# Exponentials, norm sums, weight sums and loads in other slots at the start of the second batch of a fused attention and GEGLU kernel

## The chip, the cores and the metric

The kernel runs on one core of one Trainium2 chip. The metric is the device time of one execution in microseconds, the median of several runs. The core has five engines that each work through an instruction list of their own in order: PE (TensorE, matrix products), DVE (VectorE), ACT (ScalarE), POOL (GpSimd) and SP (SyncE, here the issuer of most DMA transfers). They wait for each other on semaphores.

## The reference

An efficient attention (softmax over the features for q, over the sequence for k) feeds a GEGLU feed-forward block. Cut to what is computed:

```python
# q, k, v: (8, 8, 576, 64); w_gate, w_val: (512, 1536); w_out: (1536, 512)
q_s = exp(q - max(q, -1)) / (sum over the last axis + 1e-9)
k_s = exp(k - max(k, 2))  / (sum over the sequence + 1e-9)
kv  = einsum('bhsd,bhse->bhde', k_s, v)
x   = einsum('bhsd,bhde->bhse', q_s, kv)     # then (8 * 576, 512)
g   = x @ w_gate
out = (0.5 * g * (1 + erf(g / sqrt(2))) * (x @ w_val)) @ w_out
```

## The kernel before

Eight batches are worked one after the other. In each, 512 of the 576 rows form a main block; the 64 rows that are left of every batch are collected in `xtr` and form one more block of 512 rows. The order of blocks is 0 to 6, then the collected block, then 7. What this document calls block b is the feed-forward work on batch b.

**Attention of one batch.** q, k and v are loaded into fp32 tiles (`ld_b`: two buffers for q, two for k, one for v). ACT takes `exp` of q into `eq` and of k into `ek` (L178; two buffers each, by the parity of the batch). Each of four head pairs of `eq` is then normalised by `norm`: DVE sums and takes a reciprocal (`norm_sum`, L196 and L198), and POOL or DVE multiplies (`norm_mul`, L215). `cast_v` turns v into fp16 (L154 on POOL). `unit_kv` or `unit_kv4` forms k times v on PE. The normalised q has to be transposed: in batches 0 and 1 by PE (`unit_t`), with the left rows by a DMA (`unit_trem`, L337, tile `eqtr`), and from batch 2 by one DMA transpose of all of `eq` (`unit_td`, L344, tile `eqt`). `unit_x` or `unit_x4` multiplies with kv into PSUM tiles `psx` and `psxr`, and ACT and DVE copy these to `xt` and `xtr` (L156, L158).

**Feed-forward of one block.** Twelve tiles (`fi` 0 to 11) of 128 hidden features each: four matmuls into `psg` and four into `psv` (L425), then `gate`: Gelu on ACT (L430, into one of three buffers `gl`) and a product on DVE (L431, into `ht`). Six PSUM banks go round in a ring for `psg` and `psv`. In blocks 0 and 1 the first two or three tiles are interleaved with the last work on `xt` (`ffn_first0`, `ffn_first`): their first two matmuls of each product need only head pairs 0 and 1.

The product with w_out in blocks from 1 on is a Strassen form (`out_strassen`, L546): seven half-size products, which need sums of blocks of w_out (`tw[1]` to `tw[4]`, made once by `sum_w`, L515, on DVE) and of `ht` (`sum_h`, L532, for each block, on DVE, made between the tiles from 7 on). Product 1 uses `ht` tiles 0 to 5, product 2 uses 6 to 11, products 5 and 6 use sums, product 4 is the last before the next block's tiles.

**What sets the order.** `plan` is a table written out by hand: `at(b, FI, i, ...)` hangs work behind tile i of block b, `at(b, NS, i, ...)` at places in the product with w_out, and `ride` runs it there. What hangs there is put into the lists of the engines at that place, and so a plan entry sets the order on each engine, but not across them. SP's list holds loads, transposes and stores in order too, so that a transfer which has to wait (for a buffer to come free, or for its source) keeps the later ones waiting.

**Tables of ACT.** Gelu and Exp do not share a table. Wherever ACT changes from one to the other an ACT_TABLE_LOAD appears in the trace. `preload` (L420) runs the function on one element, to bring its table in early.

**Around the change.** In the kernel before, ACT changes to Gelu at the end of block 0's product with w_out (`at(0, NS, 7, preload)`). In block 1, tile 3 is followed by w_out sums 3 and 4, Exp of q2 (q of batch 2) and norm 0 of batch 2; tiles 4 to 6 by norms 1 to 3; tile 7 by the first half of Exp of k2 and the casts of v2; tile 9 by the DMA transpose of batch 2; tile 11 by the loads of q, k and v of batch 3, the second half of Exp of k2, Exp of q3 and k3, `exp_rem0` (Exp of batch 0's left rows) and the casts of v3. w_out sums 1 and 2 stand inside `ffn_first`.

Of the kernel before, what the change touches and what calls it, by code (L numbers as in the profile page):

```python
# [11 lines left out]
ACTF = mybir.ActivationFunctionType  # L12
ALU = mybir.AluOpType
# [5 lines left out]
def kernel(  # L19
# [10 lines left out]
    nc = tc.nc  # L30

    B, H, S, D = q.shape
# [4 lines left out]
    NFI = F // P  # L37
# [469 lines left out]

    tw = {}

    def sum_w(i):  # L510
        t = wstp.tile([P, NO, 256], f16, name=f"tw{i}", tag="wst")
        b11, b12 = wo_sb[:, 0:NO, 0:256], wo_sb[:, 0:NO, 256:512]
        b21, b22 = wo_sb[:, NO:NFI, 0:256], wo_sb[:, NO:NFI, 256:512]
        a, b = {1: (b12, b11), 2: (b22, tw.get(1)), 3: (b22, b12), 4: (b21, tw.get(2))}[i]
        nc.vector.tensor_tensor(out=t, in0=a, in1=b, op=ALU.subtract)  # L515
        tw[i] = t

    sh = {}
# [203 lines left out]
    FI, NS = 0, 1  # L722
    plan = {}

    def at(b, kind, i, *fns):
        plan.setdefault((b, kind, i), []).extend(fns)

    L = lambda f, *a: (lambda: f(*a))
# [5 lines left out]
    at(0, NS, 5, L(unit_t, 1, 0))  # L734
    at(0, NS, 16, L(unit_kv, 1, 0), L(cast_v, 1, 4, 8), L(load_batch, 2, ((v, "v"),)),
       L(norm, 1, 3))
    at(0, NS, 17, L(unit_x, 1, 0, "act", True), L(unit_x, 1, 1, "act", True))
    at(0, NS, 7, L(preload, ACTF.Gelu))
    first1 = [[L(unit_t, 1, 1), L(unit_kv, 1, 1)], [L(unit_x, 1, 2, "act"), L(sum_w, 1)],
              [L(unit_x, 1, 3, "dve"), L(sum_w, 2)]]  # L740

    def x_upper0():
        unit_x(0, 2, "act")
# [3 lines left out]


    at(1, FI, 2, L(unit_trem, 1))
    at(1, FI, 3, L(sum_w, 3), L(sum_w, 4), L(exp, "q", 2), L(norm, 2, 0, "pool"))  # L750
    at(1, FI, 4, L(norm, 2, 1, "pool"))
    at(1, FI, 5, L(norm, 2, 2, "pool"))
    at(1, FI, 6, L(norm, 2, 3, "pool"))
    at(1, FI, 7, L(exp, "k", 2, 0, 4), L(cast_v, 2, 0, H))
    at(1, FI, 9, L(unit_td, 2))
    at(1, FI, 11, L(load_batch, 3), L(exp, "k", 2, 4, 8), L(exp, "q", 3), L(exp, "k", 3), L(exp_rem0), L(cast_v, 3, 0, H))
    at(1, FI, 4, make_s)
    at(1, NS, 2, L(unit_kv4, 2))
    at(1, NS, 4, L(unit_x4, 2, ("act", "dve"), 1))
    at(2, FI, 7, L(norm_rem0))  # L760
    at(3, FI, 8, L(unit_trem, 0))
    for b in range(2, B):
        if b + 2 < B:
            at(b, FI, 0, L(load_batch, b + 2, ((v, "v"), (q, "q"), (k, "k"))))
            at(b, FI, NFI - 1, L(exp, "q", b + 2), L(exp, "k", b + 2))
            vcast = L(cast_v, b + 2, 0, H)
        if b + 1 < B:
            n = b + 1
            for hp in range(HP):
                at(b, FI, hp, L(norm_sum, n, hp), L(norm_mul, n, hp, "pool"))  # L770
            at(b, FI, 4, L(unit_td, n))
            if n + 1 < B:
                at(b, FI, 4, vcast)
            if n == 3:
                at(b, FI, 5, L(unit_kv4, n))
            at(b, NS, 4, L(unit_x4, n, ("act", "dve"), 0 if n == 4 else None))
            if n + 1 < B:
                at(b, NS, 4, L(unit_kv4, n + 1, n == 4))
# [67 lines left out]
```

## Time and profile before

The median of three runs is 308.58 us (308.30 to 308.87). The profiled execution spans 309.0 us at a mean granted PE clock of 0.994.

| engine | busy us | share of the span | instructions |
|---|---|---|---|
| PE | 295.9 | 96% | 2077 |
| DVE | 204.1 | 66% | 392 |
| ACT | 146.0 | 47% | 195 |
| POOL | 74.3 | 24% | 83 |

The page of a profile gives such totals, a strip of the span in 40 slices, the chain of work that ended last and the costliest groups of instructions. Further views are drawn from the trace: a timeline (start, duration, engine, line, operation, what it writes and reads, count, and in brackets the idle time ahead of it with what ended it), a table by stretches of time (for each stretch its length, the busy time of PE, weight load, DVE, ACT and POOL with the count of instructions, the granted PE clock, the share of the DMA engines and GB/s), and the list of waits. Where PE is busy nearly everywhere, as here, the reader looks for the stretches where it is not, or where its clock is below 1.00, and asks in the timeline what it waited for there. Block 0's product with w_out ends at about 48.6 us, block 1's tiles run from there to about 71.4, its product with w_out to about 83.7, and block 2 follows.

### The profile page before, as it was taken

The numbers are of one execution on the slowest core, as the hardware profiler recorded it, in microseconds if no ns is written. First come the engines' busy times: TensorE is split into PE (matmuls) and PEld (weight loads), VectorE is DVE, ScalarE is ACT, GpSimd is POOL, SyncE is SP. The second block draws the span as 40 slices with busy tenths as digits, with TensorE's granted clock in tenths as the row PEclk, the third lists the DMA queues.
The fourth block names the chain that finished last, engine by engine and source line by source line (L and its number), as shares of the span: only waits on it lengthen the run. The fifth ranks groups of instructions, "written<-read, shape, count | busy, mean of one in ns | idle before, by whom it ended". The sixth has DMA issues, their size and how long they took to land.

```text
span 309.0 us, 5369 instructions
## 1 busy us (share of the span) xinstructions
PE 295.9 (96%) x2077; PEld 167.6 (54%) x2077; DVE 204.1 (66%) x392; ACT 146.0 (47%) x195; POOL 74.3 (24%) x83
## 2 busy tenths in 40 slices
PE   3999999998889999999999999999999999999994
PEld 1444455445634486448644764477447644774473
DVE  2944388789737785868586848685868545834672
ACT  3763465994663385338533844384431333123320
POOL 2667461073058000720063005400510000000000
PEclk9999999999979999999999999999999999999999
DMA  6999999709959303980399029801140110022003
GB/s 224 372 383 392 401 387 387 210 0 227 379 175 377 71 0 138 367 187 0 124 345 215 1 102 341 240 0 77 61 85 3 81 57 0 0 69 69 1 2 136
DMA packets 54762, 51.66 MB, mean 167 GB/s; under 512 B 18513, under 2 KB 50769, under 8 KB 54737
## 3 DMA queue, kind: packets, MB, share of 16 engines
q1 hardware_dynamic: 53152, 49.75, 49.9%
q10 hardware_dynamic: 1584, 1.57, 1.6%
q8 instruction: 16, 0.26, 0.4%
q14 instruction: 10, 0.07, 0.1%
HBM read 37.75 MB, written 9.44 MB: 153 GB/s over the span
## 4 chain that ended last, share of the span: by engine, by line
PE 89%; DMA 5%; POOL 1%; SPq 1%; ACT 1%; DVE 1%; issue 1%; POOLq 0%; ACTq 0%
PE psg L425 30%; PE psv L425 30%; PE psa L546 12%; PE psc L546 6%; PE psy L493 3%; PE psb L546 3%; DMA vt<-in_v_dram 3%; DMA qt<-in_q_dram 2%; PE pskv L301 1%; SPq L134 1%; POOL v L154 1%; PE pst L326 1%; PE psx L388 1%; PE psx L367 1%; POOL eq L215 1%
## 5 line engine op out<-in xcount | busy, mean ns | idle before, releaser
L431 DVE SCALAR_TENSOR_TENSOR ht<-psv,gl 128x512 f16<-128x512 f32 x108 | 73.7, 685 | 67.6 <-PE psv L425 49.1
L430 ACT ACTIVATE gl<-psg 128x512 f32<-128x512 f32 x108 | 63.3, 598 | 98.1 <-PE psg L425 96.5
L425 PE MATMUL psg<-xt,wg_sb 128*128 128x512 f16 x384 | 101.6, 382 | 2.0 <-ACT xt L156 1.9
L425 PE MATMUL psv<-xt,wv_sb 128*128 128x512 f16 x384 | 101.4, 382 | 0.5 <-DVE ht L431 0.5
L425 PEld LDWEIGHTS <-wv_sb 128*128 128x128 f16 x432 | 42.4, 98 | 52.0 <-issue 2.2
L425 PEld LDWEIGHTS <-wg_sb 128*128 128x128 f16 x432 | 42.3, 98 | 51.7 <-issue 3.5
L215 POOL TENSOR_TENSOR eq<-eq,rrq 128x640 f16<-128x640 f16 (+1 forms) x27 | 34.4, 1276 | 125.6 <-issue 92.3
L546 PEld LDWEIGHTS <-ht 128*128 128x128 f16 x384 | 37.1, 98 | 8.6 <-DVE ht L431 1.5
L196 DVE TENSOR_REDUCE rq<-eq 128x10 f32<-128x640 f16 x28 | 22.7, 810 | 2.9 <-ACT eq L178 2.9
L546 PE MATMUL psa<-tw,ht 128*128 128x256 f16 x192 | 23.6, 273 | 0.2 <-DVE yo L578 0.2
L154 POOL CAST v<-vt 128x640 f16<-128x640 f32 x26 | 18.5, 754 | 14.7 <-DMA vt<-in_v_dram 14.7
L178 ACT ACTIVATE eq<-qt 128x2560 f16<-128x2560 f32 (+2 forms) x10 | 18.5, 1864 | 6.5 <-DMA qt<-in_q_dram 6.4
L178 ACT ACTIVATE ek<-kt 128x1280 f16<-128x1280 f32 (+1 forms) x11 | 19.1, 1748 | 5.0 <-DMA kt<-in_k_dram 5.0
L546 PEld LDWEIGHTS <-sh 128*128 128x128 f16 x192 | 18.8, 98 | 2.2
L628 ACT ACTIVATE yo<-psa 128x512 f32<-128x512 f32 (+1 forms) x8 | 4.6, 570 | 19.4 <-PE psa L546 19.4
L546 PE MATMUL psb<-wo_sb,ht 128*128 128x256 f16 x96 | 12.1, 273 | 1.0 <-DVE ht L431 0.9
L572 DVE TENSOR_SCALAR sn<-psa 128x512 f32<-128x512 f32 (+1 forms) x16 | 10.5, 654 | 3.9 <-PE psa L546 3.9
L425 PE MATMUL psg<-xtr,wg_sb 128*128 128x512 f16 x48 | 12.3, 379 | 0.0
L425 PE MATMUL psv<-xtr,wv_sb 128*128 128x512 f16 x48 | 12.3, 379 | 0.0
L546 PE MATMUL psc<-wo_sb,s 128*128 128x256 f16 x96 | 11.8, 273 | 0.0
L546 PE MATMUL psa<-tw,sh 128*128 128x256 f16 x96 | 11.8, 273 | 0.0
L546 PE MATMUL psa<-wo_sb,ht 128*128 128x256 f16 x96 | 11.8, 273 | 0.0
(86 smaller groups left out, 251.4 us busy)
## 6 DMA issues: line engine op xcount, KB each, us to landing
out_dram<-yo SPq DMA_DIRECT2D x15, 512.0 KB, 3.5
kt<-in_k_dram SPq DMA_DIRECT2D x7, 640.0 KB, 8.3
vt<-in_v_dram SPq DMA_DIRECT2D x7, 640.0 KB, 5.3
qt<-in_q_dram SPq DMA_DIRECT2D x7, 640.0 KB, 6.8
qt<-in_q_dram SPq DMA_DIRECT2D x8, 512.0 KB, 7.3
wost<-in_moe_w_out_dram SPq DMA_DIRECT2D x6, 512.0 KB, 7.9
kt<-in_k_dram SPq DMA_DIRECT2D x6, 512.0 KB, 9.2
vt<-in_v_dram SPq DMA_DIRECT2D x6, 512.0 KB, 5.9
```

The source lines that it names most:

```text
L134: (nc.scalar if b == 0 and t == 1 else nc.sync).dma_start(out=tiles[(nm, b)][t:P:2, h0:h1, c0 * D:NC * D], in_=src[b, h0:h1].rearrange("h ...
L154: nc.gpsimd.tensor_copy(out=dst, in_=src)
L178: nc.scalar.activation(out=dst[:, n0:NC, h0 * D:h1 * D].rearrange(o, d=D, **({"t": 2} if b >= QUAD else {})), in_=heads(tiles[(nm, b)], b, ...
L196: nc.vector.reduce_sum(rq, e, axis=mybir.AxisListType.X)
L215: (nc.gpsimd if eng == "pool" else nc.vector).tensor_tensor(out=e, in0=e, in1=rrq.unsqueeze(-1).to_broadcast((P, n, 2, D)), op=ALU.mult)
L425: nc.tensor.matmul(ps, w[:, ci, fi * P:(fi + 1) * P], xt[:, ci, :], start=(ci == 0), stop=(ci == HP - 1))
L430: nc.scalar.activation(out=gl, in_=psg, func=ACTF.Gelu)
L431: nc.vector.scalar_tensor_tensor(out=ht[:, fi, :], in0=psv, scalar=_H_SCALE, in1=gl, op0=ALU.mult, op1=ALU.mult)
L493: nc.tensor.matmul(psy, ht[:, fi, ns * P:(ns + 1) * P], wo_sb[:, fi, :], start=(fi == 0), stop=(fi == NFI - 1))
L546: nc.tensor.matmul(ps[t], a, w, start=(first and j == 0 and (t == ts[0] or ps[t].tensor is not ps[ts[0]].tensor)), stop=(j == NO - 1), ski ...
L572: nc.vector.tensor_scalar(out=sn[:, t], in0=src, scalar1=1.0 / _H_SCALE, scalar2=None, op0=ALU.mult)
L628: nc.scalar.activation(out=yo[1][:, t, c[0]], in_=src, func=ACTF.Copy, scale=1.0 / _H_SCALE)
```

## The change

Work on batches 2 and 3 that rides in block 1 is put into other slots:

- Exp of q2 takes the place of the Gelu preload at the end of block 0, while the Exp table is still in; the preload goes behind the copy of head pair 2 in `ffn_first`.
- Norms 0 and 1 of batch 2 go into `ffn_first`, norms 2 and 3 behind tiles 3 and 4.
- Sums 1 and 3 of w_out go to POOL, at the end of block 0; sums 2 and 4 stay on DVE, behind tiles 5 and 6.
- q and k of batch 3 are loaded from tile 3 of block 1 instead of tile 11; v of batch 3 stays at tile 11.
- The two halves of Exp of k2 go behind tiles 4 and 8 (before: 7 and 11), the casts of v2 behind 5, the transpose of batch 2 behind 8.
- Exp of batch 0's left rows goes from the end of block 1's tiles to the end of block 2's, and its norm from tile 7 of block 2 to tile 5 of block 3.

It is meant to have batch 3's q and k in place before ACT wants them, and to take work out of block 1's tiles.

```diff
-    def sum_w(i):
+    def sum_w(i, eng="dve"):
...
-        nc.vector.tensor_tensor(out=t, in0=a, in1=b, op=ALU.subtract)
+        (nc.gpsimd if eng == "pool" else nc.vector).tensor_tensor(out=t, in0=a, in1=b, op=ALU.subtract)
...
-    at(0, NS, 17, L(unit_x, 1, 0, "act", True), L(unit_x, 1, 1, "act", True))
-    at(0, NS, 7, L(preload, ACTF.Gelu))
-    first1 = [[L(unit_t, 1, 1), L(unit_kv, 1, 1)], [L(unit_x, 1, 2, "act"), L(sum_w, 1)],
-              [L(unit_x, 1, 3, "dve"), L(sum_w, 2)]]
+    at(0, NS, 17, L(unit_x, 1, 0, "act", True), L(unit_x, 1, 1, "act", True), L(sum_w, 1, "pool"),
+       L(sum_w, 3, "pool"))
+    at(0, NS, 7, L(exp, "q", 2))
+    first1 = [[L(unit_t, 1, 1), L(unit_kv, 1, 1)],
+              [L(unit_x, 1, 2, "act"), L(preload, ACTF.Gelu), L(norm, 2, 0, "pool")],
+              [L(unit_x, 1, 3, "dve"), L(norm, 2, 1, "pool")]]
...
     at(1, FI, 2, L(unit_trem, 1))
-    at(1, FI, 3, L(sum_w, 3), L(sum_w, 4), L(exp, "q", 2), L(norm, 2, 0, "pool"))
-    at(1, FI, 4, L(norm, 2, 1, "pool"))
-    at(1, FI, 5, L(norm, 2, 2, "pool"))
-    at(1, FI, 6, L(norm, 2, 3, "pool"))
-    at(1, FI, 7, L(exp, "k", 2, 0, 4), L(cast_v, 2, 0, H))
-    at(1, FI, 9, L(unit_td, 2))
-    at(1, FI, 11, L(load_batch, 3), L(exp, "k", 2, 4, 8), L(exp, "q", 3), L(exp, "k", 3), L(exp_rem0), L(cast_v, 3, 0, H))
-    at(1, FI, 4, make_s)
+    at(1, FI, 3, L(norm, 2, 2, "pool"), L(load_batch, 3, ((q, "q"), (k, "k"))))
+    at(1, FI, 4, L(exp, "k", 2, 0, 4), L(norm, 2, 3, "pool"), make_s)
+    at(1, FI, 5, L(sum_w, 2), L(cast_v, 2, 0, H))
+    at(1, FI, 6, L(sum_w, 4))
+    at(1, FI, 8, L(exp, "k", 2, 4, 8), L(unit_td, 2))
+    at(1, FI, 11, L(load_batch, 3, ((v, "v"),)), L(exp, "q", 3), L(exp, "k", 3), L(cast_v, 3, 0, H))
     at(1, NS, 2, L(unit_kv4, 2))
     at(1, NS, 4, L(unit_x4, 2, ("act", "dve"), 1))
-    at(2, FI, 7, L(norm_rem0))
+    at(3, FI, 5, L(norm_rem0))
...
-            at(b, FI, NFI - 1, L(exp, "q", b + 2), L(exp, "k", b + 2))
+            at(b, FI, NFI - 1, L(exp, "q", b + 2), L(exp, "k", b + 2), *([exp_rem0] if b == 2 else []))
```

## The prediction, made before the change was run

> **What bounds the kernel now.** I read the page first: PE is busy 296 of 309 us, so only idle PE, or PE at a lower clock, can give time back. Its row of slices and the clock row beneath show where (a slice is 309.0/40 = 7.72 us):
>
> ```profile
> PE   3999999998889999999999999999999999999994
> PEclk9999999999979999999999999999999999999999
> ```
>
> Slices 9 to 11 (70 to 93 us) hold the only 8s after the start, and slice 11 the only low clock. The table by stretches, with PE busy as its second number and the clock as the third from the end, resolves them:
>
> ```profile
> 68.00:72.00 4.00, 3.55 (x20) 1.78 (x19) 3.97 (x6) 2.80 (x5) 4.00 (x5) 1.00 0.57 106
> 72.00:76.00 4.00, 3.01 (x27) 2.23 (x25) 3.86 (x10) 1.78 (x2) 0.29 (x1) 1.00 0.93 221
> ...
> 84.00:85.70 1.70, 0.00 (x0) 0.00 (x0) 0.33 (x1) 1.70 (x6) 0.22 (x1) 1.00 0.50 202
> 85.70:87.00 1.30, 1.14 (x5) 0.48 (x5) 0.00 (x0) 0.97 (x2) 1.30 (x3) 1.00 0.02 9
> 87.00:89.00 2.00, 2.00 (x7) 0.69 (x5) 0.00 (x0) 1.87 (x2) 1.21 (x2) 0.54 0.55 223
> 89.00:91.00 2.00, 2.00 (x7) 0.75 (x6) 1.63 (x3) 0.61 (x2) 0.00 (x0) 0.60 0.57 115
> ```
>
> Two losses. The first is the end of block 1's tiles: the PE timeline has psv of tile 11 waiting for DVE ht near 70.1 and psb waiting for the last ht near 74.3. Tile 11 began at 69.08; with 1.73 us for a tile, 1.31 for product 1 and 10 x 0.109 ahead of psb's last pair, that pair was due at 73.21 and began at 75.15: **1.94 us**. The second is the passage to block 2. There product 4 ends near 83.73 (82.42 + 12 x 0.109), but four groups of block 2, at 0.864 each, end only at 91.15 instead of 83.73 + 3.46 = 87.19: **3.96 us**, of which about 2.0 idle, 0.15 a second short wait, 1.8 half clock.
>
> Who causes the passage? The ACT timeline:
>
> ```profile
> 78.39 2.34 ACT L178 ACTIVATE eq<-qt 128x2560 f16<-128x2560 f32 x1 [4.60 <-DMA qt<-in_q_dram]
> 81.95 2.34 ACT L178 ACTIVATE ek<-kt 128x2560 f16<-128x2560 f32 x1 [1.22 <-DMA kt<-in_k_dram]
> 84.19 0.61 ACT L223 ACTIVATE eq0r<-q0r 64x512 f16<-64x512 f32 x1
> 84.71 0.51 ACT L156 CAST xtr<-psxr 128x128 f16<-128x128 f32 x2
> 85.12 1.06 ACT L156 CAST xt<-psx 128x512 f16<-128x512 f32 x2
> ```
>
> The xt copies that start block 2 stand behind Exp of q3 and k3, which wait for their loads. Those loads are late because the DMA queue stands behind a transposing DMA, and that behind batch 2's norms:
>
> ```profile
> 68.80 3.08 SPq L344 DMA_TRANSPOSE eqt<-eq  x1
> 71.93 1.29 SPq L134 DMA_DIRECT2D qt<-in_q_dram  x2
> 73.27 1.66 SPq L134 DMA_DIRECT2D kt<-in_k_dram  x2
> 75.03 1.94 SPq L134 DMA_DIRECT2D vt<-in_v_dram  x2
> ```
>
> The chain of waits names vt in this stretch; the timeline decides, since the Exps wait for qt and kt.
>
> **What the Trainium skill says.** "TensorE: Matmul & The Clock Gate", What's actually happening: half rate after an idle window of about 3.4 us, full rate after as much busy time. The trace agrees on half (0.50 between 88 and 90 us) and on the recovery (about 3.6 us); here about 2 us of idleness was enough. "ScalarE: Activation LUTs", What ACT_TABLE_LOAD costs: 1283 ns plus a drain of about 1380. The trace shows 1.28 us and the next ACTIVATE at once, so I count 1.28. "GPSIMD Engine Reference", 4.1 Engine selection: two-input elementwise work is about 2x slower than on DVE. The rows show 1.26 against 0.82 us for norm's product. The same page, 1 Specifications: the SBUF interface is shared with DVE instructions that have two SBUF inputs. The trace agrees: the sums of ht (L532) take 0.42 us from 100 to 240, but 1.12, 0.82 and 0.94 beside POOL work at 67.9 to 71.7.
>
> **The change part by part.**
>
> *q and k of batch 3 queued at tile 3.* Their buffers were last read by Exp of q1 and k1, done at 47.1, so SP issues them right after the eqtr transpose (52.8 to 54.2). The DMA engines are full until 58.3 and idle until 68.8, so 2.36 MB at the 386 GB/s seen there take 6.1 us: landed near 64.5. The Exps then follow tile 11's Gelu: 71.7 + 1.28 + 2 x 2.34 = 77.7, well before the first psxr (81.6). exp_rem0 (0.61) leaves this point; at block 2's end ACT waited 2.44 for psxr, which hides it. ACT is ready for xt, and DVE's two xt copies end at 84.33 against a need at 83.73 + 3 x 0.215 = 84.38: nothing left, or 0.1. With the idle gone I expect the clock to stay up, as between blocks 2 and 3. **Gain 3.9.**
>
> *Exp of q2 in the place of the Gelu preload.* ACT is free at 49.45, but q2's second half was issued at about 42.7 and took
>
> ```profile
> qt<-in_q_dram SPq DMA_DIRECT2D x1, 512.0 KB, 7.4
> ```
>
> so it lands at 50.1, and Exp runs 50.3 to 52.6. Behind it on ACT stands the copy of psx for head pair 2 (51.80 before): it ends near 53.2, and PE wants it at 52.68. **Loss 0.55.** On DVE norm sum 0 waits for the same Exp (52.6 + 0.81 + 0.22 = 53.7), then the xt copy of pair 3 ends at 54.4; PE, already late, wants it at 54.5. The preload (1.28 + 0.20) ends at 54.7, before gate 0 needs it (54.39 + 0.55). The count of table loads from 49 to 88 us stays seven.
>
> *Sums 1 and 3 on POOL.* 1536 elements at 1.26/640 us each: 3.0 us (estimate; the GPSIMD page's 4497 ns for 2048 fp32 gives 3.4). Two from 48.8 end at 54.8 to 55.6. Beside them DVE mostly reads PSUM or one SBUF input; norm 3 of batch 1 (1.16, already beside POOL) may grow by 0.3, but the wait for q2 absorbs that. Queued behind on POOL: norms 0 and 1 (to 57.3), norm 2, norm 3 (to 62.3: ht4 60.2 on DVE, 1.03 for its sum, 1.26 on POOL), cast of v2 (to 65). No PE work asks for these before 78. DVE loses 2 x 0.95 us of work.
>
> *Sums 2 and 4 after tiles 5 and 6.* DVE idles for Gelu 5 until 63.7 (next part). From there four ht at 0.65, sums 2 and 4 at 0.95, two pairs of ht sums (0.85, 0.75) end at 69.8: before ht9 can start at 70.5. Nothing.
>
> *Exps of k2 after tiles 4 and 8.* Each costs ACT 2 x 1.28 + 1.27 = 3.83 us against 1.73 us of PE per tile, and ACT spends 0.6 a tile, so the first is caught up by tile 8. PSUM holds three tiles, so no psg waits; the first ends at 63.1. The second: Gelu 8 ends at 66.1, Gelu 9 starts at 69.95. DVE then has ht9 (70.5), two sums (0.80), ht10 (0.62), two sums (0.67), ht11: done 70.5 + 3.5 = 74.0. PE wants it at 73.21 + 0.55 = 73.76: a wait of 0.24 if nothing disturbs the sums.
>
> *v of batch 3.* It still stands behind the transpose (62.3 now) and the cast of v2. Before, q3, the first thing after the transpose, landed 9.4 us after the transpose's issue, so v3 lands at about 71.7 and POOL casts it until 75, beside exactly those sums. One sum at 0.94 instead of 0.42 adds 0.5; if v3 lands a microsecond earlier, up to 1.6; later than 73.5, nothing. I take 0.5: ht11 at 74.5 instead of 75.15, **gain 0.65**, with the q2 loss and all else ahead of it inside (1.15 at best with that loss, -0.45 at worst).
>
> *norm_rem0 and the rest.* 1.54 us of DVE move from tile 7 of block 2 to tile 5 of block 3, where norms 0 to 3 have finished; the transpose that needs it is issued after tile 8. Nothing, as DVE ran through the same in block 2 without a PE stall.
>
> **Sum.** 0.65 + 3.96 - 0.1 = 4.5: 308.6 - 4.5 = **304.1**. From block 2 on, the order of work is as before, and nothing in it waited for what moves.
>
> **The rivals.** (a) *Undisturbed*: q2 lands in time and v3 after the tight sums: ht11 at 74.0 - 0.55 = 73.45, gain 1.7 + 3.9 = 5.6, **303.0**. For it: the landing is known to 0.2 us only. (b) *The wait is handed on*: q2 costs 1.0 and v3's cast 1.6, ht11 at 74.0 + 0.45 + 1.6 = 76.05: -0.9 + 3.9 = 3.0, **305.6**; the stretched sums near 68 us speak for it. (c) *The clock falls anyway*, because the waits near 53 and 74 or the thin 64x64 matmuls suffice: 4.5 - 1.8 = 2.7, **305.9**. Against it: the waits near 74 left it at 1.00 before. (d) *Slower*: ACT is in order, and Exp of q2 now stands ahead of block 1's first Gelu. If it started 5 us later than I compute (the queue is full until 58.3), PE would idle some 5.5 us and run cold for another 1.8, and the ht waits would stay: 308.6 - 3.9 + 7.3 = **312**. Against it: the 7.4 us above.
>
> **How the numbers follow.** My forecast 0.55, (a) 0.18, (b) 0.14, (c) 0.09, (d) 0.04. The range of 302.8 to 306.1 takes in (a) to (c), with 0.2 beyond the outer two for the repeat scatter (308.3 to 308.87), and leaves out (d) and halves of the tails. Faster 0.95, within 0.2% 0.01, slower 0.04.
>
> **What would show it.** PE at 1.00 clock and without a gap over 0.2 us where block 2 begins; Exp of q3 and k3 back to back from 72 us with no DMA wait; one PE wait of about 0.5 us for ACT xt near 52.7; sums of w_out on POOL at 3 us; ht11 done near 74.5 us, with L532 rows stretched beside the cast of v3. The forecast is wrong if the passage keeps its low clock, or if PE waits over 1 us in block 1's first three tiles.

## The result, and the profile after

The changed kernel takes **307.15 us** (306.90 to 307.24), against 308.61 us for the kernel before beside it: a ratio of 0.9952, with a 95% interval of 0.9935 to 0.9969. It is faster, by 1.46 us, but that is a third of the 4.5 us that were forecast (304.1), and the time lies outside the range of 302.8 to 306.1.

The strips of the page of after answer to those of before; a slice is now 305.4/40 = 7.64 us:

```profile
PE   3999999999999999999999999999999999999994
PEclk9999999999999999999999999999999999999998
```

The three 8s and the 7 of the clock row are gone. (The new 8 at the end of the clock row costs nothing: it lies behind 302 us, where PE has no work left.) The spans seem to say that 309.0 - 305.4 = 3.6 us were won, but the times say 1.46. Setting each profiled execution's span against its own time explains it: an execution is timed some 1.8 us above its span (307.19 for the 305.4 of after), and the execution of before whose trace the prediction was read from was timed at 310.83 us, 2.2 above the median of its own kernel. This trace cannot be compared with that of after as it stands; experiment e1 has a typical one.

Block 1's end in after, on the PE timeline (start, duration, instruction, count, and in brackets the idle time with what ended it):

```profile
74.20 0.39 PE L546 MATMUL psb<-wo_sb,ht 128*128 128x256 f16 x2 [0.25 <-DVE ht L431]
74.43 1.47 PE L546 MATMUL psc<-tw,sh 128*128 128x256 f16 x12
76.11 1.47 PE L546 MATMUL psa<-tw,sh 128*128 128x256 f16 x12 [0.21 <-DVE sn L572]
...
78.63 1.47 PE L546 MATMUL psc<-wo_sb,s 128*128 128x256 f16 x12 [0.30 <-DVE sn L572]
...
82.19 1.47 PE L546 MATMUL psa<-tw,ht 128*128 128x256 f16 x12
83.50 1.03 PE L425 MATMUL psg<-xt,wg_sb 128*128 128x512 f16 x4
...
114.17 0.82 PE L301 MATMUL pskv<-v,ek 128*64 128x65 f16 x40 [0.45 <-ACT xt L156]
```

The wait for the last ht has shrunk, and block 2 follows product 4 without a gap (82.19 + 1.31 = 83.50). Three waits in these lines are new: two for `sn` (a DVE result from a PSUM tile that PE uses again) in block 1's product with w_out, and one ahead of `pskv`, the k times v product of batch 4, at the end of block 2.

ACT and SP do what they were meant to do. In the ACT timeline Exp of q3 and k3 run back to back with no wait for a load. In the SP timeline their loads stand ahead of the transpose:

```profile
72.92 2.34 ACT L178 ACTIVATE eq<-qt 128x2560 f16<-128x2560 f32 x1
75.16 2.32 ACT L178 ACTIVATE ek<-kt 128x2560 f16<-128x2560 f32 x1
81.75 0.53 ACT L156 CAST xtr<-psxr 128x128 f16<-128x128 f32 x2 [4.26 <-PE psxr L398]
```

```profile
54.35 1.67 SPq L134 DMA_DIRECT2D qt<-in_q_dram  x2
56.06 3.22 SPq L134 DMA_DIRECT2D kt<-in_k_dram  x2
62.66 4.97 SPq L344 DMA_TRANSPOSE eqt<-eq  x1
67.73 1.29 SPq L134 DMA_DIRECT2D vt<-in_v_dram  x2
```

### The profile page after: what moved, and what is told of

Same layout as the page of the kernel before. It is cut to its first block, busy times and chain, and to the rows that moved or that the text cites. A ratio compares the mean times of both kernels' runs of the same rounds, so it can differ in the third digit from the quotient of the medians.

```text
span 305.4 us, 5368 instructions
## 1 busy us (share of the span) xinstructions
PE 294.4 (96%) x2077; PEld 167.7 (55%) x2077; DVE 201.7 (66%) x390; ACT 145.9 (48%) x195; POOL 81.6 (27%) x85
## 4 chain that ended last, share of the span: by engine, by line
PE 72%; DVE 1%; ACT 0%; issue 0%
PE psg L425 24%; PE psv L425 24%; PE psa L546 13%; PE psc L546 6%; PE psb L546 3%; PE pskv L301 1%; PE psx L388 1%; DVE yo L578 0%; PE psxr L388 0%; DVE s L532 0%; DVE sn L572 0%; ACT xt L156 0%; DVE yo L624 0%; DVE ht L532 0%; ACT xtr L156 0%
## 5 line engine op out<-in xcount | busy, mean ns | idle before, releaser
L425 PE MATMUL psg<-xt,wg_sb 128*128 128x512 f16 x384 | 100.5, 379 | 0.3 <-ACT xt L156 0.3
L154 POOL CAST v<-vt 128x640 f16<-128x640 f32 x26 | 19.3, 783 | 9.5 <-DMA vt<-in_v_dram 9.5
L156 ACT CAST xtr<-psxr 128x128 f16<-128x128 f32 (+1 forms) x8 | 2.1, 290 | 21.9 <-PE psxr L388 15.1
L417 PE MATMUL pswarm<-warm,ident 128*128 128x512 f16 x20 | 7.3, 525 | 4.9 <-ACT warm L676 4.9
```

The costliest lines, as they stand in the source:

```text
L154: nc.gpsimd.tensor_copy(out=dst, in_=src)
L417: nc.tensor.matmul(ps, ident, warm, start=True, stop=True)
L425: nc.tensor.matmul(ps, w[:, ci, fi * P:(fi + 1) * P], xt[:, ci, :], start=(ci == 0), stop=(ci == HP - 1))
```

## The experiments

### e1: the kernel before once more

No edit.

> The kernel before, unchanged, for the clock of its executions. Theory A: the half clock of 1.8 us at the passage to block 2 belonged to the one profiled execution of before (309.0 us span, 310.8 us timed, 2.2 above the median). Then most executions span about 306.8 us at a clock above 0.997, and a trace of one shows only some 2.1 us lost at the passage. Rival B: the clock falls there in every execution; then spans stay near 309 with a clock near 0.994, and the change loses its gain elsewhere.

Measured: 308.55 us (308.25 to 308.93), ratio 0.9993 (0.9981 to 1.0004). The trace is of an execution of 308.58 us: span 306.8, clock 1.000. The passage on its PE timeline:

```profile
82.40 1.47 PE L546 MATMUL psa<-tw,ht 128*128 128x256 f16 x12
85.17 1.29 PE L425 MATMUL psg<-xt,wg_sb 128*128 128x512 f16 x4 [1.29 <-ACT xt L156]
86.29 1.03 PE L425 MATMUL psv<-xt,wv_sb 128*128 128x512 f16 x4
...
88.88 1.03 PE L425 MATMUL psg<-xt,wg_sb 128*128 128x512 f16 x4
```

The three groups behind the first take 2.59 us (86.29 to 88.88), 0.86 each, so none runs at half clock, and the table by stretches has the clock at 1.00 from 68 to 96 us. In the first trace the same three groups took 4.27 us (86.88 to 91.15). Product 4 ends at 83.71; four groups should end at 87.17 and end at 88.88: the passage costs **1.71 us, not 3.96**. Theory A holds; the 2.1 us that it set for the passage were 0.4 too many. The first trace shows a kind of execution that comes up now and then: of the 80 executions of before recorded with the experiments, 4 took 310.78 to 310.86 us at a mean clock of 0.994, and none of the others more than 309.35 us.

With this trace the three can be laid side by side (start of an instruction, us):

| PE begins | before, first trace | before, e1 | after | after gained on e1 |
|---|---|---|---|---|
| psb's last pair, block 1 | 75.15 | 75.13 | 74.20 | 0.93 |
| product 3, block 1 | 78.85 | 78.83 | 78.63 | 0.20 |
| product 4, block 1 | 82.42 | 82.40 | 82.19 | 0.21 |
| tile 2 of block 2 | 91.15 | 88.88 | 86.95 | 1.93 |
| tile 0 of block 3 | 119.93 | 117.65 | 116.25 | 1.40 |
| span | 309.0 | 306.8 | 305.4 | 1.4 |

Gained: 0.93 at the last ht, 1.72 at the passage. Given back: 0.73 between psb and product 3, and 0.53 in block 2. The sum, 1.39, comes close to the 1.46 that was timed.

### e2: the loads alone

```diff
-    at(1, FI, 3, L(sum_w, 3), L(sum_w, 4), ...
+    at(1, FI, 3, L(load_batch, 3, ((q, "q"), (k, "k"))), L(sum_w, 3), L(sum_w, 4), ...
-    at(1, FI, 11, L(load_batch, 3), ...
+    at(1, FI, 11, L(load_batch, 3, ((v, "v"),)), ...
```

> Before with one part of the change alone: q and k of batch 3 queued behind tile 3 of block 1. Theory A: the idle time at the passage (2.0 + 0.15 us) goes and nothing else moves: 308.6 - 2.1 = 306.5 us, with no wait of ACT for q3 or k3. Rival B (half clock regularly lost before): 308.6 - 3.9 = 304.7 us. Rival C: the transpose of batch 2, now behind two loads in the queue, comes late and takes part of the gain: 307 to 308 us.

Measured: 306.93 us, ratio 0.9947 (0.9934 to 0.9960), a gain of 1.68, where e1's passage costs 1.71. In the PE timeline psb's last pair begins at 75.10, as in before, and block 2 follows product 4 without a gap:

```profile
82.37 1.47 PE L546 MATMUL psa<-tw,ht 128*128 128x256 f16 x12
83.68 1.03 PE L425 MATMUL psg<-xt,wg_sb 128*128 128x512 f16 x4
```

So this part gains the passage and nothing else, and alone it is no slower than the whole change.

### e3: v of batch 3 later

```diff
-    at(1, FI, 11, L(load_batch, 3, ((v, "v"),)), L(exp, "q", 3), L(exp, "k", 3), L(cast_v, 3, 0, H))
+    at(1, FI, 11, L(exp, "q", 3), L(exp, "k", 3))
-    at(1, NS, 4, L(unit_x4, 2, ("act", "dve"), 1))
+    at(1, NS, 4, L(unit_x4, 2, ("act", "dve"), 1), L(load_batch, 3, ((v, "v"),)), L(cast_v, 3, 0, H))
```

> After, with load and cast of v of batch 3 moved behind product 7 of block 1. Theory: the cast on POOL at 74.2 to 77.4 us stretched two ht sums on DVE (0.82 and 0.89 instead of 0.42 us), which made PE wait twice for sn in block 1's product with w_out. Without it the L532 rows are all at 0.42 to 0.43, both waits go, and the time is 0.5 to 0.7 us below after: about 306.5 us. Rival: the waits come from the order on DVE and stay: 307.15 us. Second rival: v of batch 3 then comes late for block 2: above 307.2 us.

Measured: 306.38 us, ratio 0.9927 (0.9915 to 0.9939), 0.77 below after. First come the POOL and DVE timelines of after in the stretch concerned, then two of the rows of L532, the sums of ht, in e3 (min/median/max in ns):

```profile
74.20 3.16 POOL L154 CAST v<-vt 128x640 f16<-128x640 f32 x4 [8.19 <-DMA vt<-in_v_dram]
```

```profile
74.17 0.42 DVE L532 TENSOR_TENSOR sh<-ht 128x512 f16<-128x512 f16 x1
74.63 0.82 DVE L532 TENSOR_TENSOR sh<-sh,ht 128x512 f16<-128x512 f16 x1
75.38 0.68 DVE L572 TENSOR_SCALAR sn<-psa 128x512 f32<-128x512 f32 x1
...
76.75 0.89 DVE L532 TENSOR_TENSOR s<-ht,sh 128x512 f16<-128x512 f16 x1
```

```profile
L532 DVE TENSOR_TENSOR sh<-sh,ht x3: 424/424/424, 68.1 to 74.7; 128x512 f16<-128x512 f16 x3
...
L532 DVE TENSOR_TENSOR s<-ht,sh x3: 415/419/419, 69.4 to 76.4; 128x512 f16<-128x512 f16 x3
```

In after, the two sums that fall beside the cast take twice their time, and the sn behind each comes late for the product that reuses its PSUM tile. With the cast at 87.7 us, no sum is stretched and both waits for sn are gone. The theory holds. e3 moves the load of v3 along with the cast; e6 below tells them apart, for there v3 is loading while these sums run, its cast comes later, and no sum is stretched.

### e4: the copy of head pair 2 on DVE

```diff
-              [L(unit_x, 1, 2, "act"), L(preload, ACTF.Gelu), L(norm, 2, 0, "pool")],
+              [L(unit_x, 1, 2, "dve"), L(preload, ACTF.Gelu), L(norm, 2, 0, "pool")],
```

> After, with the copy of psx for head pair 2 of batch 1 put on DVE, which idles from 51.7 to 52.8 us there, instead of ACT, where it stands behind Exp of q2. Theory: the PE wait for ACT xt at 53.25 us (0.47 us lost) goes, and nothing stands in its way later, as PE sets the pace of block 1's tiles: 307.15 - 0.47 = about 306.7 us. Rival: the Gelu preload, the first Gelu or the last ht (set by ACT's second Exp of k2) then ends the wait instead, and the time stays at 307.1 us; the wait of psb for the last ht grows from 0.25 to 0.7 us.

Measured: 307.06 us, ratio 0.9940 (0.9919 to 0.9961): 0.09 below after, which is within the scatter. The PE timeline of e4:

```profile
54.45 0.38 PE L425 MATMUL psg<-xt,wg_sb 128*128 128x512 f16 x1 [0.28 <-DVE xt L158]
...
74.10 0.39 PE L546 MATMUL psb<-wo_sb,ht 128*128 128x256 f16 x2 [0.25 <-DVE ht L431]
...
76.53 1.47 PE L546 MATMUL psa<-tw,sh 128*128 128x256 f16 x12 [0.73 <-DVE sn L572]
```

The wait at 53.25 is gone, but another came up at the next copy, on DVE: its list has norm sum 0 ahead of the copy of pair 3, and that sum waits for Exp of q2 as well. PE reached its product with w_out only 0.1 us earlier than in after (71.28 instead of 71.38), and psb's last pair, which waits for the last ht, began 0.1 us earlier too (74.10 instead of 74.20). The loss at sn is there too, as one wait instead of two. The rival is right on the outcome; the growing wait for ht that it named did not show, since PE was hardly earlier.

### e5 and e8: who makes PE wait at 114 us

e5 puts Exp and norm of batch 0's left rows back where they were (`exp_rem0` into `at(1, FI, 11, ...)`, `norm_rem0` into `at(2, FI, 7, ...)`). e8 leaves them and takes another PSUM buffer:

```diff
-                at(b, NS, 4, L(unit_kv4, n + 1, n == 4))
+                at(b, NS, 4, L(unit_kv4, n + 1, n in (3, 4)))
```

> After, with Exp and norm of batch 0's left rows put back in blocks 1 and 2. In after, PE waits 0.45 us ahead of the k times v product of batch 4, at 114 us. Theory: that tile's PSUM buffer has changed places in after, so that it waits for the DVE copy of the second psxr instead of the ACT copy of the first; putting the two back puts the buffer back. Then the wait goes and the time is about 306.7 us; Exp of the left rows costs nothing at the end of block 1, where ACT idles 4.3 us. Rival: the wait has to do with the work of the transition and stays, 307.15 us, or ACT comes late again at the passage, above 307.2 us.

> After, with the PSUM tile of the k times v product of batch 4 taken from the ring of six instead of the pair that psxr uses; batch 0's left rows stay in blocks 2 and 3 as in after. Theory: the 0.45 us wait at 114 us is for that buffer, so it goes here too, and the time is 306.6 to 306.7 us. Rival: it goes with the place of Exp and norm of the left rows, and stays here: 307.15 us.

Measured: e5 306.60 us, ratio 0.9948 (0.9932 to 0.9964); e8 306.67 us, ratio 0.9937 (0.9918 to 0.9956): 0.55 and 0.48 below after. (e5's ratio takes in three executions far above the rest, of which more below; its median is 0.9935 of before's.) In both traces the wait is gone; first pskv of batch 4 in e5, then in e8:

```profile
113.55 0.82 PE L301 MATMUL pskv<-v,ek 128*64 128x65 f16 x40
```

```profile
116.16 0.82 PE L301 MATMUL pskv<-v,ek 128*64 128x65 f16 x40
```

As e8 keeps the rows' work in its new places, the buffer is the cause. psxr and pskv share two PSUM buffers, which are given out when the program is built from the kernel. In after, pskv of batch 4 gets the one that the second psxr used, which DVE reads until 114.02, instead of the first, which ACT reads until 113.60:

```profile
113.33 0.27 ACT L156 CAST xtr<-psxr 128x128 f16<-128x128 f32 x1 [1.92 <-PE psxr L388]
...
113.74 0.28 DVE L158 CAST xtr<-psxr 128x128 f16<-128x128 f32 x1
```

The profile names ACT xt as the end of the wait. In the built program, what stands at pskv's first weight load is a wait for DVE's read of psxr in after, and for ACT's in before. The other kernels here agree: the wait of 0.45 us stands in after, e3, e4 and e9, where pskv has the second psxr's buffer, and in none of the rest.

e8's trace is of an execution of 309.15 us, the slowest of eleven and 2.5 us above their median, and it holds something else, on DVE and on POOL:

```profile
48.55 3.77 DVE L215 TENSOR_TENSOR eq<-eq,rrq 128x640 f16<-128x640 f16 x1
```

```profile
48.54 6.73 POOL L515 TENSOR_TENSOR tw<-wo_sb 128x1536 f16<-128x1536 f16 x2
```

In after the same product, norm 3 of batch 1, takes 1.10 us and begins ahead of POOL, which begins at 48.77:

```profile
48.39 1.10 DVE L215 TENSOR_TENSOR eq<-eq,rrq 128x640 f16<-128x640 f16 x1
```

PE waits 2.22 us for it in e8. This is what e9 tests. Of e5's 22 executions three lie well above the rest as well (309.02, 309.08 and 310.75 us), and of e7's five one (308.23). No trace was taken of these, so that they have the same cause is likely and not shown.

### e6: the loads back at tile 11

```diff
-    at(1, FI, 3, L(norm, 2, 2, "pool"), L(load_batch, 3, ((q, "q"), (k, "k"))))
+    at(1, FI, 3, L(norm, 2, 2, "pool"))
-    at(1, FI, 11, L(load_batch, 3, ((v, "v"),)), L(exp, "q", 3), ...
+    at(1, FI, 11, L(load_batch, 3), L(exp, "q", 3), ...
```

> After, with q and k of batch 3 loaded from tile 11 again, the rest of the change as it is. Theory A (only the early load removes the idle time at the passage): q3 and k3 come late, ACT is late with xt, and the 1.7 us of the passage are back: about 308.8 us. Rival B: the transpose of batch 2 is now issued at 62.7 instead of 68.8 us, so loads queued behind it start at 67.7; k3 then lands near 76 us, ACT is done with its Exp near 78.4, before the first psxr (81.3), and the passage stays clean. v3 lands behind k3, near 79, so its cast leaves the ht sums alone: 306.4 to 306.6 us, below after.

Measured: **305.79 us**, ratio 0.9898 (0.9872 to 0.9924), 1.36 below after. First the SP timeline, then the ACT timeline:

```profile
62.61 3.01 SPq L344 DMA_TRANSPOSE eqt<-eq  x1
65.67 1.31 SPq L134 DMA_DIRECT2D qt<-in_q_dram  x2
67.03 1.31 SPq L134 DMA_DIRECT2D kt<-in_k_dram  x2
68.43 2.47 SPq L134 DMA_DIRECT2D vt<-in_v_dram  x2
```

```profile
72.32 1.28 ACT L178 ACT_TABLE_LOAD   x1 [0.76 <-DMA qt<-in_q_dram]
73.61 2.34 ACT L178 ACTIVATE eq<-qt 128x2560 f16<-128x2560 f32 x1
75.85 2.32 ACT L178 ACTIVATE ek<-kt 128x2560 f16<-128x2560 f32 x1
80.97 0.53 ACT L156 CAST xtr<-psxr 128x128 f16<-128x128 f32 x2 [2.80 <-PE psxr L398]
```

The transpose leaves at 62.6 instead of 68.8 us, because the norms it waits for were moved; so the loads behind it are in time without being moved themselves. Theory A is refuted, and rival B holds, at 0.6 us less than it said. The transpose holds SP for 3.01 us here and for 4.97 in after: there the loads of q and k, 9.9 us from issue to landing for k, still kept the DMA engines at 379 GB/s between 64.5 and 65.5 us; here nothing moved when it was issued. v lands behind q and k: its cast begins at 78.3, and the sums of ht stay at 0.42. pskv of batch 4 has the first psxr's buffer again. So both losses of the table, 0.73 and 0.53, are gone.

### e7: three edits at once

> After with three edits at once: load and cast of v3 behind product 7, the copy of head pair 2 on DVE, and Exp and norm of batch 0's left rows back in blocks 1 and 2. Theory: the three costs are separate, so they add: 0.77 and 0.55 as measured one by one, 0.47 expected, together 1.8 below after: 305.4 us. Rival: the last ht of block 1 is set by ACT's Exp of k2 and not by PE, so that the start of block 1 brings nothing: 305.8 us.

The edits are those of e3, e4 and e5. Measured: 305.69 us, ratio 0.9912 (0.9878 to 0.9945), 1.46 below after. The parts as measured alone, 0.77 + 0.55 + 0.09 = 1.41, add up; the 0.47 expected of e4 was not there to be had.

### e9: norm 3 after POOL's sum has begun

```diff
-       L(norm, 1, 3))
+    at(0, NS, 6, L(norm, 1, 3))
```

> After, with norm 3 of batch 1 (sum, reciprocal, product, all on DVE) moved one place down, behind the evacuation of psy 2, so that its product starts after POOL has begun its first sum of w_out instead of 0.4 us ahead of it. Theory: a DVE product with two SBUF inputs that starts beside a running two-input instruction of POOL is held up by it (3.77 us in the trace of e8, where both began at 48.5 us, against 1.10 us in after); then it takes 3 to 4 us in most executions, PE waits 2 us or more for it at the transposes near 50 us, and the time is 309 us or more. Rival: the 3.77 us had another cause; then the product takes 0.8 to 1.2 us and the time is 307.1 to 307.5 us.

Measured: 310.06 us (309.62 to 311.72), ratio 1.0049 (1.0027 to 1.0071): 2.9 above after, and no execution near 307. The trace is of the slowest, 311.72 us. In it PE also ran at half clock behind the wait (0.50 from 54 to 56 us), which by the mean clocks (0.993 or 0.994) happened in four of the eleven executions; the median is free of that. DVE, POOL and PE:

```profile
48.92 3.67 DVE L215 TENSOR_TENSOR eq<-eq,rrq 128x640 f16<-128x640 f16 x1
```

```profile
48.82 3.10 POOL L515 TENSOR_TENSOR tw<-wo_sb 128x1536 f16<-128x1536 f16 x1
51.86 3.67 POOL L515 TENSOR_TENSOR tw<-wo_sb 128x1536 f16<-128x1536 f16 x1
```

```profile
52.65 0.40 PE L326 MATMUL pst<-ident,eq 128*128 128x128 f16 x4 [2.72 <-DVE eq L215]
```

A start 0.10 us behind POOL's instead of 0.38 ahead makes the product more than three times as long: it ends at 52.59, 0.67 after POOL's first sum (48.82 + 3.10 = 51.92), and POOL's second sum takes 0.57 more than the first. The later start alone would have moved the product's end by some 0.5 us (at 1.10 us it would end at 50.02, in after it ends at 49.49); the rest is the stretching. In after it is the other way round: the product, ahead, takes 1.10, and POOL's first sum is the longer one:

```profile
48.77 3.68 POOL L515 TENSOR_TENSOR tw<-wo_sb 128x1536 f16<-128x1536 f16 x1
52.41 3.09 POOL L515 TENSOR_TENSOR tw<-wo_sb 128x1536 f16<-128x1536 f16 x1
```

So in these traces the two do not slow each other down by a share: the one that started first goes on, and the other hardly moves until it ends. The theory holds.

### e10: all sums of w_out on DVE, on top of e6

```diff
-    first1 = [[L(unit_t, 1, 1), L(unit_kv, 1, 1)],
+    first1 = [[L(unit_t, 1, 1), L(unit_kv, 1, 1), L(sum_w, 1)],
...
-    at(1, FI, 4, L(exp, "k", 2, 0, 4), L(norm, 2, 3, "pool"), make_s)
+    at(1, FI, 4, L(exp, "k", 2, 0, 4), L(norm, 2, 3, "pool"), L(sum_w, 3), make_s)
```

The two POOL sums leave `at(0, NS, 17, ...)`.

> The kernel of e6 (after with q and k of batch 3 loaded from tile 11), with sums 1 and 3 of w_out on DVE in two places where DVE idles: sum 1 behind the kv products of batch 1 (idle 51.7 to 52.8 us), sum 3 behind norm 3 of batch 2 (idle 61.2 to 63.7 us). Theory: both are hidden, POOL is free of two-input work beside DVE's norm 3, so that product takes 0.8 to 1.1 us in every execution: 305.6 to 305.8 us, and none near 308. Rival: DVE then delays norm sum 0 or the first ht, and the time is 306 us or more.

Measured: 305.83 us (305.71 to 306.02), ratio 0.9902 (0.9878 to 0.9926), the same as e6. Sum 1 runs from 51.34 to 52.29 and sum 3 from 61.03 to 61.97, both in time in which DVE idled. So POOL was not needed for them: these slots on DVE do as well. Norm 3's product took 1.22 us, beside a cast on POOL, a little more than the 0.8 to 1.1 expected. That no sum on POOL can hold it up any more follows from there being none; as e8 had one such execution in eleven, six can't show it. The trace has one more case of what e9 shows: a product of norm on POOL that began 0.26 us behind sum 3 on DVE took 1.80 instead of 1.26 us.

```profile
61.03 0.94 DVE L515 TENSOR_TENSOR tw<-wo_sb 128x1536 f16<-128x1536 f16 x1
```

```profile
61.29 1.80 POOL L215 TENSOR_TENSOR eq<-eq,rrq 128x640 f16<-128x640 f16 x1 [0.43 <-DVE rrq L198]
```

## Why the prediction was wrong, by its own steps

**The passage** (3.96 in the sum, 1.71 in e1). This is the term that failed most: it took as recurrent what one execution had lost. Some 1.7 us of half clock (set at 1.8) and 0.56 us of idle time (block 2 began 3.33 us behind product 4's start instead of 2.77) were that execution's own. The stated span of 309.0 lay above 308.87, the longest of the times beside it, although an execution is timed above its span: the trace could be seen to be untypical before anything was run. Rival (c) asked whether the clock would fall after the change; no rival asked whether it falls in every execution of before. The mechanism was right: with the loads early, ACT is ready and the gap is gone (e2). What the prediction did not ask is whether another part would do it too. The rest of the change does, by the earlier norms and transpose (e6).

**The last ht and the cast of v3** (0.65 in the sum, 0.20 measured). The ACT steps held closely: Gelu 9 at 70.03 (69.95 forecast), last ht done at 74.14 (74.0 undisturbed). v3's cast began at 74.20, not at 71.7: the transpose held SP for 4.97 us, where the 9.4 us that the prediction took over from before contain 3.08 for it, so that v's load was issued only at 67.73 and took some 6 us. What held it was the change itself, since the early loads, set to land near 64.5, were still arriving (e6). The 0.5 us set for stretched sums thus did not fall on ht. The stretching came, on two of the next sums, and cost 0.73 through sn. That the cast would only harm ht, and nothing if later than 73.5, was the false step (e3).

**"Nothing in it waited for what moves"** (0 in the sum, 0.53 measured). The wait for pskv comes from a PSUM buffer given out differently (e5, e8). No timeline of before shows this; the waits of the program built from the changed kernel do.

**Exp of q2** (0.55 of wait; PE lost 0.48, at 53.25 where 52.77 was due). The landing (Exp began at 50.39, forecast 50.3) and the copy behind it were right. The prediction counts this loss inside the term of the last ht. Whether it reaches the last ht in full stays open, as e4 put another wait of nearly the same length in its place.

**Sums on POOL** (an estimate of 3.0 us by the row of before, and one of 3.4 by the price in the Trainium skill's "GPSIMD Engine Reference", 3.1 Elementwise — side-by-side cycle accounting, which is for fp32). Measured 3.09 for the one and 3.68 for the one beside DVE's product: the row of before was right, and 3.4 is passed only where DVE is in the way. That DVE's product would grow by 0.3 at most held in after (1.10), where it begins 0.38 us ahead of POOL; the order of start, which decides it (e9), was not asked for. The rule read from 1 Specifications, that two-input DVE work contends with POOL, was right, but the 0.3 us taken for it are far below the 2.6 that the product lost in e8 and e9.

**The clock.** The prediction read that about 2 us of idle time were enough for half clock. The length of the wait alone does not decide it: PE fell to half clock behind a wait of 1.86 us in the first trace of before and of 2.72 in e9's, and stayed at full clock behind one of 2.22 in e8's.

**What held**: seven table loads, the left rows' Exp and norm hidden as work, Exp of q3 and k3 with no wait for a load, and the clock at 1.00 where block 2 begins.

The account: of the 4.5 us forecast, 2.14 are missing at the passage (3.86 set, 1.72 gained), 0.45 at ht and sn, and 0.53 at pskv, which leaves 1.4.

## What to carry to other kernels

Before a trace is priced, set its span against the times: if it lies as far from them as here, a second trace tells which of its losses recur. When a change moves several things towards one goal, ask for each whether the goal is reached without it: here q and k came early enough once the transpose ahead of them did, and loading them still earlier only held that transpose up and brought the next transfer, and the cast that waits for it, into the busiest stretch of DVE. After a reordering, compare also which buffers and waits the built program gives to instructions that were not touched. And when a change lets two engines start within some tenths of a microsecond of each other, as norm 3 on DVE and the sums on POOL do here, look at many executions and not only at the median.

## What the runs showed of the hardware that was not expected

A DVE product with two SBUF inputs (128x640, f16) took 1.10 us when it began 0.38 us ahead of a two-input POOL instruction, which then took 3.68 instead of 3.09 us; it took 3.67 and 3.77 us when it began 0.10 and 0.01 us behind, and ended 0.7 us after POOL's. Beside a cast on POOL, which has one input, a DVE sum of two SBUF inputs that takes 0.42 us alone took 0.82 to 0.94. A transposing DMA held SP's queue for 3.01 us with idle DMA engines and for 4.97 us behind loads that were still arriving. PE stayed at full clock behind a wait of 2.22 us in one execution, and fell to half clock behind one of 1.86 us in another.
